# Attention level in one burst of eight tiles, a new beginning and a new weight decoding, in a fused attention and double MLP kernel

## Chip, cores and metric

The kernel runs on one core of one Trainium2 chip. The core has a matrix engine (TensorE, PE), three engines for elementwise work (VectorE, DVE; ScalarE, ACT; GpSimd, POOL) and a queue that issues transfers (SyncE, SP); each runs its own list of instructions in order, and they wait for each other by semaphores. On-chip memory (SBUF) and the accumulators of PE (PSUM, eight banks of 2 KB per partition) have 128 partitions. The metric is the device time of one run in microseconds (us).

## What is computed

A chunked linear attention with decay, then two MLPs on its 3072 tokens of 256 features, in float32 (the weights arrive as float64).

```python
batch, H, S, D, N, chunk = 4, 8, 768, 32, 16, 32
for c in range(S // chunk):                       # state: (batch, H, N, D), zero at first
    cum = np.cumsum(log(clip(a, 1e-06, 1.0))[chunk c], axis=-1)
    L = np.exp(cum[..., :, None] - cum[..., None, :]) * causal
    M = np.einsum('bhin,bhjn->bhij', Cc, Bc) * L
    y[chunk c] = einsum('bhij,bhjd->bhid', M, xc) + einsum('bhin,bhnd->bhid', Cc, state) * np.exp(cum)[..., None]
    state = exp(sum(la)) * state + sum_j(Bc_j xc_j * exp(cum[-1] - cum_j))
x = y.transpose(0, 2, 1, 3).reshape(3072, 256)
h = np.maximum(x @ w_in, 0.0)                     # first MLP: 256 -> 2048 -> 256
x = h * h @ w_out
h = x @ w2_in                                     # second MLP, same sizes
y = (h * np.clip(h + 3.0, 0.0, 6.0) / 6.0) @ w2_out
```

## The kernel before

**Tiles and steps.** The 3072 tokens are six tiles of 512. The attention runs in 12 levels of 64 positions for all four batches and eight heads; two levels make one tile's input (act_h and act_l, the high part in the PE's reduced format and the rest of it). The first MLP ("a") goes through the six tiles, then the second ("b"). One tile has 16 steps f, one for each 128 of the 2048 hidden features. `step` (L411) emits: `mm1` (L350), six matmuls of 128x128 by 128x512 into a bank h (high weight by high input, low weight by high, high weight by low, for two halves of the 256 features); `gate` (L362); and `mm2` (L383) of the step two back (LAG = 2), six matmuls into the two output banks y. After step 15 each output is copied to act_h on ACT (L399) and subtracted from on DVE (L400) to give act_l. Everything is scheduled by hand: each engine executes in the order in which the program emits.

**Gate.** For "a": Relu and Square on ACT, a rounding copy gh on DVE (L369), and gl = g - gh on DVE (L377). For "b": Relu(h + 3) on ACT (L372), min and multiply on DVE (L373), copy on ACT (L374), gl on DVE.

**Weights.** Each MLP has 16 blocks j of 0.5 MB, taking turns between w_in and w_out; steps 2n and 2n+1 need blocks 2n and (two steps later) 2n+1. `load_w` (L286) decodes a block: its transfer, `early` (L313, ACT copies the upper words of the float64s), two DVE operations that collect low bits and sign (L332, L334), a third that joins them (L336), and `late` (L301): the high part on ACT (L306), the low part on POOL (L307). It is a generator that the steps advance: twice a step in tile 0 for the first MLP's weights, and from tile 5 on for the second's, with three transfer buffers each.

**Attention of one level.** `scale` (POOL) multiplies B and C by the decays and lays C out by head; `tokens` (POOL) scales the token-major B; `scores` (L216) are 16 small matmuls on 32 rows; `mask` (L226, DVE) moves the causal part of them to `mt`; `outputs` (L234) has 16 matmuls C by state ("inter", L241) and 32 mask by x ("intra", L247); `update` (L252) has 16; `advance` (DVE) makes the next state from u and the decay gam; `evac` writes the level into the tile's input (ACT L280, DVE L282). These small matmuls sit four at a time in separate parts of the PE array, and a level comes to PE in three visits: scores in step 2, outputs in step 4, update in step 5 of each period of eight steps (`PLAN`, `ORDER`). While tile t is in the MLP, levels 2t+2 and 2t+3 are worked; levels 0 and 1 stand in the beginning.

**Beginning.** DVE forms the running products of the decays a (`products`), their reciprocals and corrections (`decays`, in two halves), PE spreads them over the partitions for levels 0 and 1 (`spread`, L149), and the others go through DRAM (scr). The decays of a whole level (gl) make a round trip through DRAM as well (`gammas_out`, L162 and L163), before `gammas` (L167) can run on DVE.

**Banks.** In the first MLP: one pool for the attention with two banks for scores or outputs ("cy") and one for the update, two banks for h, three for y.

The lines on which the change and the sum turn are these: the order in which a decode alternates with a step, and the banks.

```python
ps_h = ctx.enter_context(tc.tile_pool(name="ps_h", bufs=2, space=PSUM, reuse_waits="tile"))
ps_y = ctx.enter_context(tc.tile_pool(name="ps_y", bufs=3, space=PSUM, reuse_waits="tile"))
```

Of the kernel before, what the change touches and what calls it, by code (L numbers as in the profile page):

```python
# [46 lines left out]
def attn_mlp_mlp(ctx: ExitStack, tc, a, bT, cT, bK, x, w1i, w1o, w2i, w2o, yT):  # L47
# [21 lines left out]
    act_h, act_l = ([actp.tile([P, 2, TOK], F32R, tag=f"{k}{i}", name=f"act_{k}{i}") for i in range(NT)] for k in "hl")  # L69
# [8 lines left out]
    mts = [at1.tile([P, 2, 2 * G], F32, tag=f"mt{i}", name=f"mt{i}") for i in range(2)]  # L78
# [30 lines left out]
    ef = at1.tile([R0, 2, G], F32, tag="efr", name="efr")  # L109
    gs = at1.tile([R0, 3, CPG], F32, tag="gs", name="gs")  # L110

    ft = at1.tile([CH, CPG, NB, SGS, H], F32, tag="ft", name="ft")

    gl = at1.tile([P, 2, NB, NLEV], F32, tag="gl", name="gl")
    gam = at1.tile([P, 2, NB, NLEV], F32, tag="gam", name="gam")
    pr, rc = ef[:, 0, :], ef[:, 1, :]
    p4 = pr.rearrange("p (c e t) -> p c e t", e=2, t=SEG)
    r4 = rc.rearrange("p (c e t) -> p c e t", e=2, t=SEG)
    scr = dram.tile([CPG, SGS, H, 2, NB, CH], F32, tag="scr", name="scr")
    gsc = dram.tile([H, 2, NGRP, CPG], F32, tag="gsc", name="gsc")  # L120

    def products():
        nc.vector.tensor_scalar(out=av, in0=av, scalar1=1e-6, scalar2=1.0, op0=ALU.max, op1=ALU.min)
        nc.vector.tensor_copy(out=seg.rearrange("p (s t) -> p s t", t=SEG)[:, :, 0:1],
                              in_=av.rearrange("p (s t) -> p s t", t=SEG)[:, :, 0:1])
        nc.vector.tensor_tensor_scan(out=pr, data0=av, data1=seg, initial=1.0, op0=ALU.mult, op1=ALU.max)
        for i in range(2):
            nc.vector.tensor_copy(out=gs[:, i, :], in_=p4[:, :, i, SEG - 1])

    def decays(i):  # L130

        t, k = slice(i * P, i * P + P), slice(2 * i, 2 * i + 2)
        nc.vector.reciprocal(out=rc[:, t], in_=pr[:, t])
        nc.vector.tensor_copy(out=gs[:, 2, k], in_=r4[:, k, 0, SEG - 1])
        nc.vector.tensor_tensor(out=r4[:, k, 0, :], in0=r4[:, k, 0, :],
                                in1=gs[:, 0, k].unsqueeze(2).broadcast_to([R0, 2, SEG]), op=ALU.mult)
        nc.vector.tensor_tensor(out=p4[:, k, 0, :], in0=p4[:, k, 0, :],
                                in1=gs[:, 2, k].unsqueeze(2).broadcast_to([R0, 2, SEG]), op=ALU.mult)

    def decays_out(i):  # L140
        for k in (2 * i, 2 * i + 1):
            for w in range(2):
                nc.sync.dma_start(out=scr[k, :, :, w].rearrange("s h b t -> b (s h) t"), in_=ef[:, w, k * CH:k * CH + CH])

    def spread(l):

        efp = ps_s.tile([P, NB, 2, CH], F32, tag=f"efp{l}", name=f"efp{l}")
        for b in range(NB):
            nc.tensor.matmul(out=efp[:, b], lhsT=sel[:, b], rhs=ef[:, :, l * CH:l * CH + CH], start=True, stop=True)  # L149
        lev[l]["ef"] = efp.rearrange("p b w t -> p w b t")  # L150

    def f_tokens(i):

        ftp = ps_s.tile([CH, 2, R0], F32, tag="ftp", name=f"ftp{i}")
        for j in range(2):
            nc.tensor.transpose(out=ftp[:, j, :], in_=rc[:, (2 * i + j) * CH:(2 * i + j + 1) * CH],
                                identity=ident[0:R0, 0:R0])
        nc.scalar.copy(out=ft[:, 2 * i:2 * i + 2].rearrange("p k b s h -> p k (b s h)"), in_=ftp)

    def gammas_out():  # L160
        for i in range(2):
            nc.sync.dma_start(out=gsc[:, i].rearrange("h g k -> g h k"), in_=gs[:, i, :])  # L162
        nc.sync.dma_start(out=gl.rearrange("p i b l -> p (i b l)"), in_=gsc.rearrange("h i g k -> h (i g k)")  # L163
                          .unsqueeze(1).broadcast_to([H, NS, 2 * NGRP * CPG]))

    def gammas():
        nc.vector.tensor_tensor(out=gl[:, 1, :, 0:NLEV - 1], in0=gl[:, 1, :, 0:NLEV - 1], in1=gl[:, 0, :, 1:NLEV],  # L167
                                op=ALU.mult)
        for e in range(2):
            nc.vector.tensor_scalar(out=gam[:, e], in0=gl[:, 1], scalar1=hm[:, e:e + 1], scalar2=None, op0=ALU.mult)  # L170
# [380 lines left out]
```

## Time and profile before

| | |
|---|---|
| median of 3 runs | 629.55 us (627.54 to 629.99) |
| the profiled execution | 629.27 us, its span 627.6 us |
| PE busy | 588.6 us, 94% of the span |
| DVE busy | 370.8 us, 59% |
| ACT busy | 296.8 us, 47% |
| POOL busy | 100.8 us, 16% |
| moved by transfers | 34.58 MB, mean 55 GB/s |

The span is the time between the first and the last instruction of the profiled execution; busy times count instructions that compute, not waits or issues. The chain of waits is followed backwards from the last instruction, at each step to what released it, and here it is read forwards; a timeline lists every instruction of a stretch with its start; the releaser behind an arrow is what ended the idle time before it. PEclk is the clock that PE was granted, as a share of its full speed.

### The profile page before, as it was taken

What the parts mean: (1) busy time and instruction counts of PE and PEld (TensorE: products, weight loads), DVE (VectorE), ACT (ScalarE), POOL (GpSimd) and SP (SyncE); (2) the same over time, 40 slices, a digit from 0 to 9 for tenths busy, and PEclk for the clock granted to TensorE, in tenths of its full rate; (3) what the DMA queues carried; (4) which work ended last, traced back from release to release, by engine and by line L of the source; (5) the groups of instructions that cost most, each with busy time, mean ns of one, the idle gap of its engine ahead of it and who ended that gap; (6) DMA issues with size and microseconds to landing.
All of it is one profiled execution on the core that took longest, in us unless ns stands there. A gap on an engine that the chain in (4) does not pass through costs nothing.

```text
span 627.6 us, 10383 instructions
## 1 busy us (share of the span) xinstructions
PE 588.6 (94%) x4180; PEld 474.2 (76%) x4180; DVE 370.8 (59%) x589; ACT 296.8 (47%) x494; POOL 100.8 (16%) x95
## 2 busy tenths in 40 slices
PE   4646879999999999999999999999999999999997
PEld 4534657787787888878887788888888888888885
DVE  4548899645543644445389988454555555554543
ACT  1216545343444434443476666554544544545453
POOL 5143465221020120200013323000000000000000
PEclk9777899999999999999999999999999999999999
DMA  8493732113021130500024430010000100100101
GB/s 201 118 200 110 181 105 68 36 43 76 9 68 36 45 75 9 169 1 1 2 68 137 132 101 1 1 34 0 18 17 1 35 1 1 33 1 1 34 0 35
DMA packets 36081, 34.58 MB, mean 55 GB/s; under 512 B 15200, under 2 KB 30656, under 8 KB 36032
## 3 DMA queue, kind: packets, MB, share of 16 engines
q1 hardware_dynamic: 36032, 33.91, 20.7%
q8 instruction: 33, 0.54, 0.4%
q14 instruction: 16, 0.13, 0.1%
HBM read 30.56 MB, written 3.35 MB: 54 GB/s over the span
## 4 chain that ended last, share of the span: by engine, by line
PE 82%; DVE 7%; DMA 4%; issue 3%; ACT 1%; POOL 1%; SPq 1%; DVEq 0%; ACTq 0%
PE yb L394 21%; PE hb L356 21%; PE ya L394 18%; PE ha L356 17%; PE ya L247 2%; DMA rawa<-in_w1i 2%; DVE gla L377 2%; PE sc L222 1%; DMA gsc<-gs 1%; PE ya L241 1%; DVE lowa L333 1%; DVE wta L336 1%; POOL al L307 1%; DMA C<-in_cT 1%; PE u L259 1%
## 5 line engine op out<-in xcount | busy, mean ns | idle before, releaser
L366 ACT ACTIVATE ga<-ha 128x512 f32<-128x512 f32 x96 | 57.2, 596 | 127.4 <-PE ha L356 124.9
L377 DVE TENSOR_TENSOR glb<-gb,ghb 128x512 fp32r<-128x512 f32 x96 | 66.4, 691 | 60.5 <-ACT ghb L374 60.1
L373 DVE SCALAR_TENSOR_TENSOR gb<-gb,hb 128x512 f32<-128x512 f32 x96 | 66.1, 688 | 54.1 <-ACT gb L372 53.7
L374 ACT ACTIVATE ghb<-gb 128x512 fp32r<-128x512 f32 x96 | 60.8, 633 | 74.8 <-DVE gb L373 74.8
L372 ACT ACTIVATE gb<-hb,three 128x512 f32<-128x512 f32 x96 | 65.9, 686 | 51.9 <-PE hb L356 51.9
L369 DVE CAST gha<-ga 128x512 fp32r<-128x512 f32 x96 | 43.6, 454 | 74.8 <-ACT ga L367 74.8
L377 DVE TENSOR_TENSOR gla<-ga,gha 128x512 fp32r<-128x512 f32 x96 | 83.9, 874 | 6.7
L356 PE MATMUL ha<-act_h,al 128*128 128x512 f32 x192 | 77.2, 402 | 9.5 <-POOL al L307 9.5
L356 PE MATMUL ha<-act_h,ah 128*128 128x512 f32 x192 | 76.9, 400 | 7.6 <-ACT ah L306 4.8
L394 PE MATMUL ya<-gla,ah 128*128 128x512 f32 x192 | 75.8, 395 | 3.7 <-DVE gla L377 3.7
L394 PE MATMUL ya<-gha,ah 128*128 128x512 f32 x192 | 78.5, 409 | 0.0
L356 PE MATMUL ha<-act_l,ah 128*128 128x512 f32 x192 | 76.2, 397 | 0.0
L394 PE MATMUL ya<-gha,al 128*128 128x512 f32 x192 | 75.3, 392 | 0.0
L394 PE MATMUL yb<-glb,bh 128*128 128x512 f32 x192 | 74.8, 390 | 0.0
L356 PE MATMUL hb<-act_h,bl 128*128 128x512 f32 x192 | 74.7, 389 | 0.0
L394 PE MATMUL yb<-ghb,bl 128*128 128x512 f32 x192 | 74.7, 389 | 0.0
L394 PE MATMUL yb<-ghb,bh 128*128 128x512 f32 x192 | 74.7, 389 | 0.0
L356 PE MATMUL hb<-act_h,bh 128*128 128x512 f32 x192 | 74.7, 389 | 0.0
L356 PE MATMUL hb<-act_l,bh 128*128 128x512 f32 x192 | 74.7, 389 | 0.0
L367 ACT ACTIVATE ga<-ga 128x512 f32<-128x512 f32 x96 | 60.6, 632 | 3.0
L356 PEld LDWEIGHTS ha<-act_h,al 128*128 128x128 f32 x192 | 36.9, 192 | 18.8 <-POOL al L307 11.3
L356 PEld LDWEIGHTS ha<-act_h,ah 128*128 128x128 f32 x192 | 36.7, 191 | 17.7 <-ACT ah L306 6.6
(81 smaller groups left out, 745.5 us busy)
## 6 DMA issues: line engine op xcount, KB each, us to landing
x<-in_x SPq DMA_DIRECT2D x24, 256.0 KB
rawa<-in_w1i SPq DMA_DIRECT2D x8, 512.0 KB
rawa<-in_w1o SPq DMA_DIRECT2D x8, 512.0 KB
rawb<-in_w2i SPq DMA_DIRECT2D x8, 512.0 KB
rawb<-in_w2o SPq DMA_DIRECT2D x8, 512.0 KB
out_yT<-o SPq DMA_DIRECT2D x12, 256.0 KB
ef<-scr SPq DMA_DIRECT2D x10, 256.0 KB
B<-in_bT SPq DMA_DIRECT2D x12, 128.0 KB
```

The source lines that it names most:

```text
L222: nc.tensor.matmul(out=sc[r:r + CH, p // 2, b * P:b * P + P].rearrange("j (e i) -> j e i", e=2), lhsT=d["B"][q, b], rhs=d["cb"][q, :, b], ...
L241: nc.tensor.matmul(out=y[r:r + CH, p // 2, b * CH:b * CH + CH], lhsT=state["S"][q, b], rhs=d["C"][q, b], start=b == 0, stop=False, skip_gr ...
L247: nc.tensor.matmul(out=y[o:o + HD, p // 2, b * CH:b * CH + CH], lhsT=d["x"][j, b, HD * h:HD * h + HD], rhs=mts[l % 2][j, p // 2, (2 * b + ...
L356: nc.tensor.matmul(out=h, lhsT=wt[fb][:, k, fo * P:fo * P + P], rhs=xt[t][:, k, :], start=i == 0, stop=i == 5)
L366: nc.scalar.activation(out=g, in_=h, func=AF.Relu)
L367: nc.scalar.activation(out=g, in_=g, func=AF.Square)
L369: nc.vector.tensor_copy(out=gh, in_=g)
L372: nc.scalar.activation(out=g, in_=h, func=AF.Relu, bias=three)
L373: nc.vector.scalar_tensor_tensor(out=g, in0=g, scalar=6.0, in1=h, op0=ALU.min, op1=ALU.mult)
L374: nc.scalar.activation(out=gh, in_=g, func=AF.Copy)
L377: nc.vector.tensor_tensor(out=gl, in0=g, in1=gh.bitcast(F32), op=ALU.subtract)
L394: nc.tensor.matmul(out=ys[m], lhsT=terms[i][0][fb][:, fo, m * P:m * P + P], rhs=terms[i][1], start=f == 0 and i == 0, stop=f == NF - 1 and ...
```

## The change

- **Level in a burst.** `outputs` and `update` of a level and the scores of the next level become one visit to PE, `burst`, in step 4 of each eight. The operands lie so that batches 0 and 1 use rows 0 to 63 and batches 2 and 3 rows 64 to 127 (x and B of tokens in one buffer `xb` of two halves): matmuls of 32 or 64 rows stand eight at a time in the array. Inter becomes 32 matmuls of 32 columns of weights instead of 16 of 64. All results of a level lie in one buffer of four banks ("att"), so the outputs y keep two banks instead of three. `after` in step 5 has the evacuation, the next level's mask and the state. The layout of C by head moves from POOL to ACT (`heads`).
- **Beginning.** The decays of levels 0 to 2 come by a matmul (`gammas_first`), those of later levels by the round trip, taken in at step 5 of tile 0. Scores of levels 0 and 1 go together. B of levels 0 and 1 and one part of xb are issued by ACT. The decays go out to DRAM in 4 transfers instead of 8, behind their second half. Block 2 comes behind level 2's inputs, block 3 behind the write of the decays.
- **Weight decoding.** Blocks 3 to 10 land in the space of the inputs of tiles 2 to 5, which are not used yet, so that transfers run further ahead (two at each even step of tile 0). The first two of the three DVE operations now have one source each and no mixed operation (`join`). The order within a step is `decode`: join(j), early(j+1), split(j), with j = f + 3 in tile 0; for the second weights, by the table `at`, one block in two of three steps.
- **Gate of the first MLP.** Relu on ACT, g = Relu(h) times h on DVE, the rounding copy on ACT, gl on DVE: as in the second MLP.

```diff
-PLAN = {"load": (0, 0), "scale": (0, 0), "tok": (1, 0), "scores": (2, 0), "mask": (2, 0), "out": (4, 0), "upd": (5, 0),
-        "evac": (5, 0)}
+PLAN = {0: {1: ("load3",), 2: ("scale2",), 3: ("head2",), 4: ("scores2", "mask2", "tok2"), 6: ("scale3", "head3"),
+            8: ("burst2",), 9: ("evac2", "load4"), 10: ("tok3",), 11: ("scale4", "head4"), 13: ("burst3",),
+            14: ("evac3", "load5")}}
...
+        _d = {0: (f"tok{_l}",), 1: (f"scale{_l + 1}",), 2: (f"head{_l + 1}",), 4: (f"burst{_l}",),
+              5: (f"evac{_l}",), 6: (f"load{_l + 2}",)}
...
+    def gammas_first(ps):
+
+        nc.vector.tensor_tensor(out=gg, in0=gs[:, 1, 0:CPG - 1], in1=gs[:, 0, 1:CPG], op=ALU.mult)
+        gp = ps[:, 0:NB * (CPG - 1)].rearrange("p (b l) -> p b l", b=NB)
+        for b in range(NB):
+            nc.tensor.matmul(out=gp[:, b], lhsT=sel[:, b], rhs=gg, start=True, stop=True)
+        return gp
...
+    def scores(l, sc):
...
+        for c in range(2):
+            for p in range(NPR):
+                for r in range(2):
+                    q, b = slice(32 * p, 32 * p + 32), 2 * r + c
+                    nc.tensor.matmul(out=sc[CH * r:CH * r + CH, p, P * c:P * c + P].rearrange("j (e i) -> j e i", e=2),
+                                     lhsT=d["bc"][q, b, 1], rhs=d["cb"][q, :, b], start=True, stop=True)
...
+    def intra(l):
+
+        y, x = lev[l]["y"], lev[l]["xb"]
+        for c in range(2):
+            for k in range(2):
+                for r in range(2):
+                    q = slice(CH * r, CH * r + CH)
+                    for o in range(4):
+                        h = 4 * k + o
+                        p, e = divmod(h, 2)
+                        nc.tensor.matmul(out=y[HD * o:HD * o + HD, 2 * r + k, c * CH:c * CH + CH],
+                                         lhsT=x[q, c, HD * h:HD * h + HD],
+                                         rhs=mts[l % 2][q, p, (2 * c + e) * CH:(2 * c + e) * CH + CH],
+                                         start=not l, stop=True, skip_group_check=True)
...
+    def burst(l, nxt=True):
+
+        t = ps_a.tile([P, NPR, TOK], F32, tag="att", name=f"att{l}")
+        place(l, t)
+        inter(l)
+        intra(l)
+        update(l)
+        if nxt and l + 1 < NLEV:
+            scores(l + 1, t[:, :, 0:G])
+
+    def after(l):
+        evac_h(l)
+        if l + 1 < NLEV:
+            mask(l + 1, (1,))
+        advance(l)
+        evac_l(l)
+        if l + 1 < NLEV:
+            mask(l + 1, (0,))
...
+        def dma(self, j):
+            if self.pre == "a" and 3 <= j < 11:
+                t, k = 2 + (j - 3) // 2, "hl"[(j - 3) % 2]
+                raw = actp.tile([P, 2, 256, 2], U32, tag=f"{k}{t}", name=f"rawa{j}")
...
+            nc.vector.tensor_scalar(out=low, in0=self.raws[j][:, :, 1], scalar1=0x80000000, scalar2=None,
+                                    op0=ALU.bitwise_and)
+            nc.vector.tensor_scalar(out=low.bitcast(U16).rearrange("p (n z) -> p n z", z=2)[:, :, 0], in0=top,
+                                    scalar1=2.0 ** -13, scalar2=7.0, op0=ALU.mult, op1=ALU.min)
...
-            nc.scalar.activation(out=g, in_=g, func=AF.Square)
...
-            nc.vector.tensor_copy(out=gh, in_=g)
...
+            nc.vector.tensor_tensor(out=g, in0=g, in1=h, op=ALU.mult)
...
+        nc.scalar.activation(out=gh, in_=g, func=AF.Copy)
...
-    ps_y = ctx.enter_context(tc.tile_pool(name="ps_y", bufs=3, space=PSUM, reuse_waits="tile"))
+    ps_y = ctx.enter_context(tc.tile_pool(name="ps_y", bufs=2, space=PSUM, reuse_waits="tile"))
...
+    def decode(x, j):
+
+        if j < NF:
+            x.join(j)
+        if j + 1 < NF:
+            x.early(j + 1)
+        if j < NF:
+            x.split(j)
+
+    def mid_first(t, f):
+        for j in (6 + 2 * (f // 2) + i for i in range(2)) if f % 2 == 0 else ():
+            if j < NF:
+                w1.dma(j)
+        if f == 5:
+            gammas()
+        attention(t, f)
+        decode(w1, f + 3)
...
+            at = {(k * 3 + 1) // 2 + 1: k for k in range(NF)}
```

What this does to the order on three engines is shown here; a name's number only tells its instances apart.

**PE, level 4 in tile 1.** Before, behind the last `mm1` matmul of step 4 stood two sorts of small matmuls (L241 inter, L247 intra); the scores (L222) stood two steps ahead, and the update (L259) one step behind:

```order
L356 MATMUL ha_4_1236<-act_l_93,ah_538 128x512
L241 MATMUL ya_1248<-C_738,S_1059 64x64 x16
L247 MATMUL ya_1248<-mt_104,x_742 32x64 x32
L394 MATMUL ya_0_1208<-gha_2_1182,ah_493 128x512
L394 MATMUL ya_0_1208<-gha_2_1182,al_494 128x512
```

After, inter (L295), intra (L309), update (L323) and the next level's scores (L275) stand in the same place:

```order
L437 MATMUL ha_4_1278<-act_l_887,ah_506 128x512
L295 MATMUL att_1291<-bc_891,S_1144 32x64 x32
L309 MATMUL att_1291<-mt_92,xb_894 32x64 x32
L323 MATMUL att_1291<-xb_894 32x64 x16
L275 MATMUL att_1291<-cb_1246,bc_1150 64x128 x16
L471 MATMUL ya_0_1250<-gha_2_1240,ah_472 128x512
```

Update and scores moved into the one visit, and inter has twice as many matmuls of half the columns.

**ACT, steps 0 and 1 of tile 0.** L366 is the gate's Relu and L367 its Square, L306 the high part of a block (late), L315 a block's first copy (early). Before:

```order
L366 ACTIVATE ga_0_454<-ha_0_445 128x512
L367 ACTIVATE ga_0_454<-ga_0_454 128x512
L306 ACTIVATE ah_466<-wta_393 128x512
L315 ACTIVATE wta_470<-rawa_427 128x512
L366 ACTIVATE ga_1_484<-ha_1_475 128x512
```

After, with L447 the Relu, L452 the gate's rounding copy, L402 early and L421 the high part (split); block 3's early (rawa_423) stands ahead of the first Relu:

```order
L402 ACTIVATE wta_440<-rawa_423 128x512
L447 ACTIVATE ga_0_458<-ha_0_449 128x512
L452 ACTIVATE gha_0_456<-ga_0_458 128x512
L402 ACTIVATE wta_470<-rawa_425 128x512
L421 ACTIVATE ah_472<-wta_440 128x512
L447 ACTIVATE ga_1_486<-ha_1_477 128x512
```

The high part now stands behind the next block's early and belongs to the block joined in the same step, not to the one joined the step before.

**SP, the transfers from the decays on.** Before, the level decays (gsc, gl) and eight writes of scr stood ahead of block 3 (rawa_320), and level 2's inputs behind it:

```order
L162 DMA gsc<-gs 12x8x4 x2
L163 DMA gl<-gsc 128x1x96
L143 DMA scr<-efr 4x24x64 x8
L297 DMA rawa_320<-in_w1o 128x1024
L182 DMA B_404<-in_bT 128x4x64
L182 DMA C_406<-in_cT 128x4x64
L186 DMA ef_408<-scr 128x1x512
L193 DMA x_410<-in_x 64x4x256 x2
```

After, level 2's inputs and block 2 (rawa_166) have been issued already; four writes, then blocks 3 to 5, the level decays, level 2's decays and two more blocks:

```order
L396 DMA rawa_166<-in_w1i 128x1024
L156 DMA scr<-efr 4x24x128 x4
L396 DMA rawa_423<-in_w1o 128x1024
L396 DMA rawa_425<-in_w1i 128x1024
L396 DMA rawa_427<-in_w1o 128x1024
L195 DMA gl<-gsc 128x1x96
L236 DMA ef_430<-scr 128x1x512
L396 DMA rawa_462<-in_w1i 128x1024
L396 DMA rawa_464<-in_w1o 128x1024
```

The writes still stand ahead of block 3, but each carries both halves of a level's decays, and four more blocks follow without a level's inputs between them.

## Rows read from the trace of the kernel before

**Rows 1.** Chain of waits in order of time: start us, us, what.

```profile
36.96 9.93 DMA rawa<-in_w1i
...
106.89 1.36 PE ha L356 x6
...
312.31 1.36 PE ha L356 x6
...
359.01 1.37 PE hb L356 x6
...
619.09 4.09 PE yb L394 x18
```

**Rows 2.** Timeline to 50 us: start us, us, engine, line, operation, [idle before <-releaser].

```profile
5.84 2.05 PE L149 MATMUL efp<-efr,sel 96*128 96x128 f32 x8 [5.84 <-DVE efr L137]
...
19.69 5.12 SPq L143 DMA_DIRECT2D scr<-efr  x8
...
21.12 0.20 DVE L167 TENSOR_TENSOR gl<-gl 128x44 f32<-128x44 f32 x1 [4.76 <-DMA gl<-gsc]
...
28.96 0.79 PE L356 MATMUL ha<-act_h,ah 128*128 128x512 f32 x1
...
41.94 1.93 PE L222 MATMUL sc<-cblk,B 32*64 32x128 f32 x32
...
46.97 0.66 ACT L315 ACTIVATE wta<-rawa 128x512 f32<-128x512 f32 x1 [12.35 <-DMA rawa<-in_w1i]
```

**Rows 3.** The chain of waits again, level 6 in tile 2.

```profile
165.43 1.03 PE sc L222 x32
...
172.15 0.62 PE ya L241 x32
172.77 1.03 PE ya L247 x64
...
176.74 0.58 PE u L259 x32
```

**Rows 4.** Busy us by stretch: PE, PEld, DVE, ACT, POOL, PEclk, DMA share, GB/s.

```profile
40.00:42.00 2.00, 2.00 (x9) 1.06 (x9) 0.00 (x0) 0.00 (x0) 0.47 (x1) 0.50 1.10 186
90.00:100.00 10.00, 7.34 (x148) 5.45 (x148) 9.90 (x16) 5.96 (x11) 4.84 (x3) 1.00 0.22 55
```

**Rows 5.** Timeline: a tile's evacuation (164 us) and a second-MLP gate (450 us).

```profile
163.92 1.07 ACT L399 ACTIVATE act_h<-ya 128x512 fp32r<-128x512 f32 x2
...
450.06 0.39 PE L356 MATMUL hb<-act_l,bh 128*128 128x512 f32 x1
...
450.55 0.69 ACT L372 ACTIVATE gb<-hb,three 128x512 f32<-128x512 f32 x1 [0.64 <-PE hb L356]
...
451.27 0.69 DVE L373 SCALAR_TENSOR_TENSOR gb<-gb,hb 128x512 f32<-128x512 f32 x1 [0.64 <-ACT gb L372]
...
451.99 0.63 ACT L374 ACTIVATE ghb<-gb 128x512 fp32r<-128x512 f32 x1 [0.76 <-DVE gb L373]
```

**Rows 6.** Groups by line and shape: count | busy us, mean ns | idle before <-releasers.

```profile
L366 ACT ACTIVATE ga<-ha 128x512 f32<-128x512 f32 x96 | 57.2, 596 | 127.4 <-PE ha L356 124.9 <-DVE gla L377 2.4
...
L307 POOL TENSOR_TENSOR al<-wta,ah 128x512 fp32r<-128x512 f32 x16 | 27.0, 1690 | 50.8 <-ACT ah L306 50.8
...
L229 DVE COPY_PREDICATED mt<-tri,sc 128x512 f32<-128x512 uint32 x24 | 16.3, 732 | 7.8 <-PE sc L222 7.6
...
L282 DVE TENSOR_TENSOR act_l<-ya,act_h 128x256 fp32r<-128x256 f32 x24 | 9.1, 419 | 35.3 <-ACT act_h L280 35.3
...
L332 DVE TENSOR_SCALAR lowa<-rawa 128x512 uint32<-128x512 uint16 x16 | 7.5, 470 | 0.1
...
L133 DVE RECIPROCAL efr<-efr 96x128 f32<-96x128 f32 x2 | 1.9, 936 | 0.0
```

**Rows 7.** Timeline at 331 us, GpSimd and VectorE.

```profile
330.96 1.81 POOL L307 TENSOR_TENSOR bl<-wtb,bh 128x512 fp32r<-128x512 f32 x1 [3.03 <-ACT bh L306]
...
331.54 1.78 DVE L377 TENSOR_TENSOR gla<-ga,gha 128x512 fp32r<-128x512 f32 x1
```

More of the change, by code (lines that the diff above doesn't have):

```diff
@@ L145, in spread, with decays_out @@
-    def spread(l):
-        efp = ps_s.tile([P, NB, 2, CH], F32, tag=f"efp{l}", name=f"efp{l}")
+    def decays_out():
+        for k in (2, 3, 0, 1):
+            nc.sync.dma_start(out=scr[k].rearrange("s h b w t -> b (s h) (w t)"),
+                              in_=ef[:, k].rearrange("p w t -> p (w t)"))
+    def spread(l, efp):
         for b in range(NB):
-            nc.tensor.matmul(out=efp[:, b], lhsT=sel[:, b], rhs=ef[:, :, l * CH:l * CH + CH], start=True, stop=True)
-        lev[l]["ef"] = efp.rearrange("p b w t -> p w b t")
@@ L454, in attn_mlp_mlp @@
-    decays_out(1)
-    scores(0)
-    mask(0)
-    update(0)
-    outputs(0, ps_s, "ya0")
-    gammas()
-    next(w1)
-    scores(1)
-    advance(0)
-    evac(0)
-    mask(1)
-    next(w1)
-    outputs(1)
-    update(1)
-    next(w1)
-    evac(1)
-    advance(1)
-    for l in (2, 3):
-        load(l)
-        load_x(l)
-    next(w1)
-    next(w1)
+    gammas_first2(gp)
+    sc = ps_a.tile([P, NPR, TOK], F32, tag="att", name="att_s")
+    scores(0, sc[:, :, 0:G])
+    scores(1, sc[:, :, G:])
+    w1.early(0)
@@ new lines, in attn_mlp_mlp @@
+    mask(0, (0, 1))
+    mask(1, (0, 1))
+    place(0, ps_s.tile([P, 4, TOK], F32, tag="big", name="yu0"))
+    update(0)
+    intra(0)
+    advance(0)
+    evac_h(0)
+    w1.join(0)
+    w1.split(0)
+    w1.early(1)
+    evac_l(0)
+    burst(1, False)
+    evac_h(1)
+    w1.join(1)
+    evac_l(1)
+    advance(1)
+    decays(1)
+    decays_out()
+    f_tokens(1, ps_s.tile([P, 4, TOK], F32, tag="big", name="ftb")[:, 2])
+    w1.split(1)
+    w1.early(2)
+    for j in (3, 4, 5):
+        w1.dma(j)
@@ L476, in attn_mlp_mlp @@
+    gammas_in()
+    load_ef(2)
+    w1.join(2)
+    w1.split(2)
+    w1.early(3)
     start_ctx.close()
     ps_h = ctx.enter_context(tc.tile_pool(name="ps_h", bufs=2, space=PSUM, reuse_waits="tile"))
-    ps_y = ctx.enter_context(tc.tile_pool(name="ps_y", bufs=3, space=PSUM, reuse_waits="tile"))
+    ps_y = ctx.enter_context(tc.tile_pool(name="ps_y", bufs=2, space=PSUM, reuse_waits="tile"))
     yps, hps = [ps_y], [ps_h]
-    does = {"load": lambda l: l + 2 < NLEV and (load(l + 2), load_x(l + 2)), "scale": lambda l: scale(l, nc.gpsimd),
-            "tok": tokens, "scores": scores, "mask": mask, "out": outputs, "upd": lambda l: (update(l), advance(l)),
-            "evac": evac}
@@ L484, in attn_mlp_mlp, with first_scores @@
-    PLAN["load"] = (6, 0)
-    def mid(t, f):
-        l, i = 2 * t + 2 + f // 8, f % 8
-        if l < NLEV:
-            for nm in ORDER:
-                if PLAN[nm][0] == i:
-                    does[nm](l)
+    def first_scores(l):
+        sc = ps_a.tile([P, NPR, TOK], F32, tag="att", name=f"att_s{l}")
+        scores(l, sc[:, :, 0:G])
+    does = {"load": load_all, "scale": scale, "head": heads, "tok": tokens, "scores": first_scores, "mask": mask,
+            "burst": burst, "evac": after}
@@ L493, in attn_mlp_mlp @@
     w2 = None
+    at = {}
     for t in range(NT):
```

373 lines of the change are left out of this document (198 added, 175 removed).

## The prediction

> **What bounds the kernel now.** I read the chain of waits first [rows 1]: where TensorE (PE) never waits it is pieces of six matmuls of 1.36 us, so a step (first matmul group and second) is 2.72 us, a tile of 16 steps 43.5, and the 192 steps of both MLPs 522. The same view gives borders: tile 1 begins at 106.89, tile 5 at 312.31, the second MLP at 359.01, the last 18 matmuls end at 623.18; the first MLP matmul starts at 28.96 [rows 2]. So the span of 627.6 is 29.0 of beginning, 77.9 for tile 0 (34.4 above 43.5), 205.4 for tiles 1 to 4 (31.3 above 174.1), 46.7 for tile 5 (3.2 above), 264.2 for the second MLP (97 steps are 263.8: nothing to gain) and 4.4 of end. The run took 629.27, 1.67 more than its span; I sum against that run, and the median, 629.55, is 0.28 above it.
>
> In tiles 1 to 4 the excess is the attention's own matmuls: per level pieces of 1.03, 0.62, 1.03 and 0.58 [rows 3], 3.26 together, and 0.7 that three visits to another tile shape cost: 31.3 is seven levels of 4.0 and the last, which has no update, of 3.1. In tile 0 it is the weights: ScalarE (ACT) idled 12.35 us before it could copy block 4 [rows 2], whose transfer took 9.93 [rows 1], and step 1's Relu stood behind that copy, so not before 47.5. The granted clock is part of it: 0.50, 1.2 GHz, at 40 to 42 us, 1.00 at 90 to 100 with PE busy 7.3 of 10 [rows 4].
>
> **The change part by part.**
>
> *Burst.* The small matmuls are bound by streaming through four tiles, not by their issue: 64 of 64 columns take 1.03, 32 take 0.58, so one more costs 14 ns; with 128 columns it is twice that [rows 3]; and at 1.2 GHz the scores took 1.93 [rows 2, 4]. Eight tiles at a time therefore halve scores (0.52), intra (0.52) and update (0.29); inter has twice the matmuls at twice the width: 0.62. Sum 1.95, plus one visit (0.22) and two changes of shape inside (0.06 to 0.1 each): 2.3 where 4.0 stood, and 1.45 for 3.1 in the last level. Tiles 1 to 4: 7 x 2.3 + 1.45 = 17.6 instead of 31.3, so -13.7. The bound on the other side: no more than four tiles ever ran, so no row shows eight; were 14 ns an issue limit, scores, intra and update would stay and inter would double to 1.07: 4.1 a level and 2.4 for the last, 31.1 in all, so -0.2.
>
> [...]
>
> *Two output buffers instead of three* (the burst needs four PSUM banks). At the start of tiles 1 to 4 the first second-MLP-group matmul must wait until the previous tile's output 0 is evacuated. From the gate's timeline [rows 5], counted from the last matmul start of step 1 (there 450.06): Relu begins at +0.49 and, with the first MLP's 0.60 [rows 6], ends at +1.09, multiply (0.69) at +1.81, copy (0.63) at +2.47, the subtraction gl, as long as the multiply, at +3.19; the evacuating subtraction stands behind gl on VectorE (DVE), 0.69 more: +3.9. PE would be there at +0.23 + 1.36 + 1.36 = +2.95. So a stall of 0.95 and 0.1 to restart, four times: +4.2. Output 1 is free just in time. Between 0 (if evacuation overtook the gate; the order forbids it) and 8.
>
> *Beginning.* Matrix gammas replace the DMA round trip for which DVE idled 4.76 [rows 2]; scores for two levels go together. But the second spread waits for f_tokens and the gamma matmuls: the first ends at 5.84 + 2.05 [rows 2], 16 records between them at 0.13 to 0.26 each (a spread's eight take 2.05) are 2.1 to 4.1, I take 2.5, the second spread 2.05, scale 0.69, two gamma operations 0.5: 13.6. From there DVE works in a row: four masks of 0.73, an advance of 0.42, two joins of 1.55, four evacuations of 0.42, a second advance 0.85, a reciprocal 0.94 and three small operations of the second decays, 0.7 [rows 6]: 2.9 + 0.4 + 3.1 + 1.7 + 0.85 + 1.6 = 10.6, and about 1.3 for waits: the second decays end at 25.5 (22.5 to 27.5). What is queued behind them: on PE f_tokens and then the first MLP matmul, at about 26.5 against 28.96. On SP the four scr writes (0.64 each, 2.6 [rows 2]), and behind them block 3. It is issued at 28.1; alone it should land 3.6 later (between 2.5, its 0.5 MB at 200 GB/s, and 9.93 [rows 1]). On ACT block 3's copy (0.67, estimated from L366's 0.60) stands ahead of the first Relu: Relu 0 at 32.4, Relu 1 one loop later, some 11 us before today's 47.5.
>
> *Decode loop of tile 0.* In steps 0 to 12 ACT has Relu(f), copy(f), early, split of block f+3, Relu(f+1); DVE has multiply(f), the three join operations, gl(f). Split waits for the join, and the next Relu stands behind split: a loop that no lead of PE shortens. Relu 0.60 [rows 6], multiply 0.69 [rows 5], join 0.42 + 0.42 + 0.69 [rows 5, 6], three hand-overs 0.1 and gaps 0.06, and 0.53 from split's start to the next Relu's (two ACT operations 1.07 [rows 5]): 3.5. GpSimd's subtraction for the block (1.69 [rows 6]) starts as split ends and runs till 1.85 after the Relu began; the join's first operation is due at 1.32. A DVE operation that comes while GpSimd runs may wait: gla took 1.78 instead of 0.69 and ended 0.55 after the POOL operation [rows 7]. So 3.5 to 4.1; I take 3.8, since most operations of the nearest kind (L332, mean 0.47 [rows 6]) did not wait. [...]
>
> 13 steps: 49.4. Attention in the loop on DVE: two masks of 0.73 in step 4, three small gamma operations in step 5 (0.6), and in step 9 two masks, four operations of 0.42 (advance and low parts): 1.5 + 0.6 + 3.1 = 5.2. Three scales and two token products on POOL, hitting DVE for 0 to 1.1 each: 3.0. From Relu 13 to tile 1: mm2 11 to 13, mm1 14 and 15 and the evacuation at step 14 ahead of gl: 5.3. Tile 1 begins at 32.4 + 49.4 + 5.2 + 3.0 + 5.3 = 95.3, 11.6 earlier (88 to 104).
>
> *Second weights.* The same order is used in 16 of 24 steps from tile 5 on. Of three steps two decode: 3.5 and, behind the other's POOL operation, 3.8; the third needs only Relu, multiply and copy, 1.95. 9.25 against 8.16 of PE: 1.1 lost in each of eight groups, 8.7, plus two tile evacuations in the chain, 1.3 each; about 3 is hidden by the lead that gl has over its use. +7.5 (3 to 11) replaces today's 3.2 to 3.5: +4.1.
>
> At nothing: the gate's new operations (ACT and DVE have the same sum, and 1.3 of 2.72 busy; without that cover 0.1 per step), head masks on ACT, the evacuation in step 5 of a level: 2.9 of DVE ahead of gl, which is due 3 us later; if that cover went, up to 0.7 in each of eight levels.
>
> **Sum.** 95.3 + (205.4 - 13.7 + 4.2 = 195.9) + (46.7 + 264.2 + 4.1 = 315.0) + 4.4 = 610.6; with 1.67 around it 612.3.
>
> **Rivals.** *Eight tiles don't overlap*: the burst costs 4.1 and 13.5 come back: 625.8. For it: nothing ever ran more than four. Against: time follows columns and clock. *The loop is quicker*: no POOL collision (13 x 0.3 + 3.0), block 3 lands at 30 and the second weights hide: 612.3 - 3.9 - 3.0 - 1.7 - 4 = 600. *The join meets GpSimd twice* (the slower side): in every block, of both MLPs, not only the first but also the last join operation waits 1.1, because GpSimd's subtraction comes late; 29 blocks x 1.1 = 32: 644, slower than now from 0.7 a block on. Against: GpSimd is idle from 1.85 on until the join is done, except for five scales and products. *The clock stays at 1.2 GHz in tile 0*: steps of 5.44 instead of 3.8, 13 x 1.64 = 21: 633.6. For it: 0.50 after idle stretches [rows 4]; against: with PE busy for 7.3 of 10 it was 1.00, and here it is 2.72 of 3.8.
>
> **How the numbers follow.** Forecast 612.3 with 0.62, quicker loop 0.17, no overlap 0.10, join twice 0.05, slow clock 0.06. The range leaves out the two slow cases and the tails of the others: the unknown terms (loop +-4, transitions +-4, second weights +-4, beginning +-3) give 603 to 622 around the forecast, and I reach to both neighbours: 601 to 625. A measurement of this kernel tells 0.5% (3.1 us) from no change: faster means below 626.4, slower above 632.7. Faster takes forecast, quicker loop and half of no overlap (it lies on that bound): 0.84; same its other half and a third of the slow clock: 0.07; slower the rest: 0.09.
>
> **What would show it.** Right: a burst of 2.3 us with scores of about 0.5; tile 1 beginning near 95; Relu 0 behind block 3's copy at about 32 and Relus 3.8 apart; a PE wait of about 1 us on act_l at the start of tiles 1 to 4; 7 us of waits at the second weights. Wrong: small matmuls still 14 ns apart, a step in tile 0 that PE sets (2.72), or blocks that come later than the loop asks.

## The result and the profile after

The changed kernel takes 638.13 us (median of 4 runs, 635.36 to 640.41) against 629.77 us for the kernel before on the same chips (4 runs): a ratio of 1.0146, 95% interval 1.0108 to 1.0183. It is slower by 8 us (1.1 to 1.8%) where I forecast 17 us less, and it lies outside the range of 601 to 625. The profiled execution took 636.95 us with a span of 635.2.

Three lines of the page of the changed kernel: busy time of each engine, shares of the chain of waits by engine, and the queue that carries instructions (packets, MB, share of 16 engines).

```profile
PE 583.9 (92%) x4552; PEld 467.5 (74%) x4552; DVE 363.0 (57%) x590; ACT 304.2 (48%) x521; POOL 69.3 (11%) x73
...
PE 64%; DVE 15%; ACT 6%; issue 6%; DMA 4%; SPq 3%; POOL 1%; DVEq 0%; ACTq 0%; POOLq 0%
...
q8 instruction: 35, 0.57, 0.4%
```

PE is busy 5 us less than before, so the small matmuls did get shorter, and yet its share of the chain fell from 82% to 64%: DVE has 15% (7% before), and 6% (3%) stand under "issue", waiting for which the profile names nobody. The borders, from the timeline (start us, us, engine, line, operation, [idle before <-releaser]):

```profile
29.46 0.79 PE L437 MATMUL ha<-act_h,ah 128*128 128x512 f32 x1 [0.57 <-ACT ft L174]
...
99.15 0.50 PE L437 MATMUL ha<-act_h,ah 128*128 128x512 f32 x1 [0.17 <-ACT act_h L349]
...
315.62 0.39 PE L437 MATMUL ha<-act_h,ah 128*128 128x512 f32 x1
...
362.36 0.39 PE L437 MATMUL hb<-act_h,bh 128*128 128x512 f32 x1
```

These answer to [rows 1, 2]. The last matmul ends at 630.83.

| part | before | predicted | after |
|---|---|---|---|
| first MLP matmul starts | 28.96 | 26.5 | 29.46 |
| tile 1 begins | 106.9 | 95.3 | 99.15 |
| tiles 1 to 4 | 205.4 | 195.9 | 216.5 |
| tile 5 and second MLP | 310.9 | 315.0 | 315.2 |
| end | 4.4 | 4.4 | 4.4 |

So the miss of 24.6 us in the span is 3.9 before tile 1 and 20.6 in tiles 1 to 4.

**Tiles 1 to 4, by step.** A step without attention is 2.72; the four tiles have 42.4 us above that, where I expected 21.8. By the starts of the steps they are: 20.9 for the eight bursts where nothing disturbs them (2.73 each, 1.79 for the last); 8.3 for gaps inside or right behind four of the bursts, and 0.9 for a slow clock after one of them; 5.1 for a wait in the third step behind the burst, where gl of the step next to it is used; 4.6 for the start of each tile; 2.4 for a backlog that tile 0 leaves to tile 1. A disturbed burst, that of level 6, in the chain of waits (start us, us, what), which answers to [rows 3]:

```profile
168.36 0.79 PE att L295 x53
169.15 0.79 PE att L309 x53
169.93 0.31 PE att L323 x22
170.25 2.05 issue
172.30 0.70 PE att L275 x32
```

Inter 0.79, intra 0.79, update 0.31, and then PE does nothing for 2.05 us before the scores. The other gaps of that kind in these tiles, from PE's timeline:

```profile
144.68 0.40 PE L471 MATMUL ya<-gha,al 128*128 128x512 f32 x1 [0.90 <-issue]
...
251.63 0.44 PE L275 MATMUL att<-cb,bc 32*64 32x128 f32 x5 [1.71 <-issue]
...
279.44 0.31 PE L323 MATMUL att<-xb 64*32 64x64 f32 x6 [1.98 <-issue]
```

They come at different instructions: behind the burst of level 5, between update and scores at level 6, between two scores at level 9, between two update matmuls at level 10; levels 4, 7, 8 and 11 have none. Operands hardly explain a gap in the middle of one group. Counting every instruction of PE in the trace from the start (weight loads, matmuls and the 48 of its sequencer, most of them waits for semaphores), the gaps stand at instructions 3009, 3521, 5313 and 5825, and one of 1.0 us in the beginning at 705: all distances are multiples of 256. The instruction queue of the page moved 0.57 MB in 35 pieces, 16 KB each, for some 9,150 instructions: one piece for about 260. The trace has the time of each piece (us), and counted from the start the 11th, 13th, 20th and 22nd belong to the gaps:

| level | instruction | its piece | PE goes on | behind the piece's end |
|---|---|---|---|---|
| 5 | 3009 | 142.29 to 143.23 | 144.68 | 1.44 |
| 6 | 3521 | 169.44 to 170.88 | 172.30 | 1.42 |
| 9 | 5313 | 249.35 to 250.28 | 251.63 | 1.35 |
| 10 | 5825 | 276.72 to 278.00 | 279.44 | 1.44 |

Each of these pieces begins only 0.7 to 1.4 us after PE has passed the place 256 instructions earlier. Wherever in tiles 1 to 4 PE crosses such a place without a gap, the piece had ended 2.7 us or more before.

A burst of inter, intra, update and scores is 384 records (loads and matmuls) in 2.5 us. Where one such place falls into its first third, the next falls inside the burst or right behind it, 1.5 to 1.8 us later by PE's records at the four gaps, before its piece is there. At level 7 a place falls right at the burst's start; there the next piece began at 193.50, ahead of the burst at 195.7, and no gap came.

### The profile page after: what moved, and what is told of

It reads as the page before. It is cut to its first block, busy times and chain, and to the rows that moved or that the text cites. A ratio compares the mean times of both kernels' runs of the same rounds, so it can differ in the third digit from the quotient of the medians.

```text
span 635.2 us, 11105 instructions
## 1 busy us (share of the span) xinstructions
PE 583.9 (92%) x4552; PEld 467.5 (74%) x4552; DVE 363.0 (57%) x590; ACT 304.2 (48%) x521; POOL 69.3 (11%) x73
## 4 chain that ended last, share of the span: by engine, by line
PE 64%; DVE 15%; ACT 6%; issue 6%; DMA 4%; SPq 3%; POOL 1%; DVEq 0%; ACTq 0%; POOLq 0%
PE yb L471 19%; PE hb L437 19%; PE ya L471 11%; PE ha L437 11%; DVE ga L448 3%; DVE mt L283 2%; DVE gla L454 2%; ACT ga L447 2%; ACT gha L452 2%; DMA rawa<-in_w1o 2%; DVE wtb L411 1%; PE att L295 1%; PE att L309 1%; DVE act_l L354 1%; DVE lowb L409 1%
## 5 line engine op out<-in xcount | busy, mean ns | idle before, releaser
L452 ACT ACTIVATE gha<-ga 128x512 fp32r<-128x512 f32 x96 | 60.8, 633 | 99.8 <-DVE ga L448 99.8
L448 DVE TENSOR_TENSOR ga<-ga,ha 128x512 f32<-128x512 f32 x96 | 65.7, 685 | 73.3 <-ACT ga L447 72.7
L452 ACT ACTIVATE ghb<-gb 128x512 fp32r<-128x512 f32 x96 | 60.9, 634 | 72.9 <-DVE gb L451 72.9
L454 DVE TENSOR_TENSOR gla<-ga,gha 128x512 fp32r<-128x512 f32 x96 | 67.8, 707 | 44.8 <-ACT gha L452 44.8
L471 PE MATMUL ya<-gla,ah 128*128 128x512 f32 x192 | 78.1, 407 | 9.7 <-DVE gla L454 9.5
L447 ACT ACTIVATE ga<-ha 128x512 f32<-128x512 f32 x96 | 56.7, 591 | 52.1 <-PE ha L437 52.1
L471 PEld LDWEIGHTS ya<-gla,ah 128*128 128x128 f32 x192 | 36.7, 191 | 25.1 <-DVE gla L454 16.6
```

Of the source, the lines that this page charges most:

```text
L447: nc.scalar.activation(out=g, in_=h, func=AF.Relu)
L448: nc.vector.tensor_tensor(out=g, in0=g, in1=h, op=ALU.mult)
L452: nc.scalar.activation(out=gh, in_=g, func=AF.Copy)
L454: nc.vector.tensor_tensor(out=gl, in0=g, in1=gh.bitcast(F32), op=ALU.subtract)
L471: nc.tensor.matmul(out=ys[m], lhsT=terms[i][0][fb][:, fo, m * P:m * P + P], rhs=terms[i][1], start=f == 0 and i == 0, stop=f == NF - 1 and ...
```

## Experiments

**Is it the supply of instructions?** The first experiment moves only the count of instructions.

```diff
     spread(1, efp)
+    for i in range(32):
+        q = slice(32 * (i % 4), 32 * (i % 4) + 32)
+        nc.tensor.matmul(out=big[q, 2, 256:288], lhsT=ident[q, q], rhs=ident[q, q], start=True, stop=True)
     scale(0, nc.vector)
```

> The changed kernel with 32 extra matmuls of 32x32 in the beginning, written to an unused part of a bank; they shift every later PE instruction by 128 records (two loads and two matmuls each). Theory A: PE's instructions come in blocks of 256, and a burst that uses up one block within about 3 us waits for the next; the gaps without a releaser then move from the bursts of levels 5, 6, 9 and 10 to those of levels 4, 7 and 8 (1 to 2 us each; level 5 at most 0.5). Theory B: the scores at the burst's end wait for their operands (the laid out C, the scaled B); the gaps then stay at levels 5, 6, 9 and 10. Time by A within 3 us of the changed kernel, by B the same plus up to 1 us.

639.52 us in a single run. PE's timeline of this kernel at the bursts of levels 4, 5, 7 and 8:

```profile
119.98 0.43 PE L275 MATMUL att<-cb,bc 32*64 32x128 f32 x3
121.89 0.69 PE L275 MATMUL att<-cb,bc 32*64 32x128 f32 x29 [1.48 <-issue]
...
147.74 0.69 PE L275 MATMUL att<-cb,bc 32*64 32x128 f32 x32
...
201.53 0.37 PE L275 MATMUL att<-cb,bc 32*64 32x128 f32 x2 [1.54 <-issue]
...
230.60 0.42 PE L323 MATMUL att<-xb 64*32 64x64 f32 x3 [1.93 <-issue]
```

Levels 4, 7 and 8 now have the gap, levels 5, 6, 9 and 10 none; the gaps stand at instructions 2497, 4289 and 4801, the same remainder of 256 as before, and PE goes on 1.37 to 1.50 us behind the end of a piece. Two more came in tile 0, at levels 2 and 3 (1.59 and 1.02) and at the same remainder, which I had not worked out. Apart from 1 us that the padding adds to the beginning, nothing but the count was changed ahead of these bursts, so theory A holds, and theory B falls.

**Fewer records in a row.** The cure that follows is to leave the next piece more time: inter and intra in step 4, update and scores in step 5. This kernel also moves a part of DVE's work from step 5 to step 6 (the next one moves a similar part, and nothing else).

```diff
         intra(l)
+        if not nxt:
+            update(l)
+        lev[l]["t"] = t
+
+    def after(l):
         update(l)
-        if nxt and l + 1 < NLEV:
-            scores(l + 1, t[:, :, 0:G])
-
-    def after(l):
+        if l + 1 < NLEV:
+            scores(l + 1, lev[l]["t"][:, :, 0:G])
         evac_h(l)
+        evac_l(l)
+
+    def rest(l):
         if l + 1 < NLEV:
-            mask(l + 1, (1,))
+            mask(l + 1)
         advance(l)
-        evac_l(l)
...
```

> The kernel with the spread work (the first mask and the state also in step 6, the low parts in step 5) and with a level's burst in two visits: inter and intra in step 4, update and the next level's scores in step 5. Theory A (blocks of 256 instructions): 256 and 128 records with a step between them use up at most one block in 3 us; the gaps in the bursts go (8.3 us in tiles 1 to 4 down to under 1.5), eight more visits cost 0.25 to 0.3 each, 2.2, and the late gl goes as in the kernel with the spread work alone: 11 to 12 us less than the changed kernel, total about 627. Theory B (operands): the scores come 2.7 us later, so their gap shrinks too, but the gaps at the update (level 10) and behind the burst (level 5) stay: 630 to 632.

624.76 us, ratio to the kernel before 0.9925 (0.9892 to 0.9959). That is 8.6 less than the kernel that moves DVE's work alone (633.39, ten runs of each), so the second visit, and not the moved work, brought most of that. Level 6 in its chain of waits:

```profile
166.05 0.78 PE att L295 x53
166.83 0.79 PE att L309 x53
167.62 1.58 PE ya L474 x6
...
170.58 0.39 PE att L323 x32
170.97 0.62 PE att L275 x32
```

No gap is left in any level of tiles 1 to 4; a level costs 1.79 + 1.25 = 3.04 everywhere, 0.31 for the second visit, and no wait stands in the third step behind it. That is 2 us better than expected; the slow clock behind the gaps went as well (1.00 from 100 to 300 us). That clock, in the changed kernel, by the view of stretches (columns as in [rows 4]):

```profile
277.00:279.40 2.40, 0.46 (x47) 0.30 (x31) 0.74 (x2) 0.63 (x1) 0.00 (x0) 1.00 0.00 0
...
282.00:285.00 3.00, 3.00 (x10) 2.29 (x9) 0.00 (x0) 0.00 (x0) 0.00 (x0) 0.61 0.00 0
```

PE was busy 0.46 of 2.40 us there (level 10's gap), and from 282 to 285 the granted clock was 0.61 with PE busy throughout (0.50 from 281 to 284, 1.00 from 284.5); that cost 0.9. Behind the gaps of levels 5, 6 and 9 it stayed at 1.00.

**The wait behind a burst.** In the changed kernel, the chain behind level 4's burst:

```profile
122.33 0.64 ACT gha L452
122.97 0.54 ACT act_h L349 x2
...
123.53 0.75 DVE mt L283
...
124.95 0.75 DVE act_l L354 x2
125.70 0.66 DVE mt L283
126.36 1.00 DVE gla L454
127.36 0.04 issue
127.40 1.20 PE ya L471 x4
```

gl of step 5 stands behind two masks, the state and the low parts on DVE, and these behind the evacuation copies on ACT, which stand behind the gate's rounding copy. PE waits for gl. At three of the seven levels gl itself, 0.69 alone, took 0.4 to 0.5 longer while GpSimd worked, here beside the next level's tokens:

```profile
126.18 0.61 POOL L264 TENSOR_TENSOR xb<-xb,ft 128x256 f32<-128x256 f32 x1
...
126.25 1.09 DVE L454 TENSOR_TENSOR gla<-ga,gha 128x512 fp32r<-128x512 f32 x1
```

At a fourth, level 6, an operation of the state took 0.69 instead of 0.43 in the same way. These meetings are 1.6 of the 5.1; at the three levels without one PE waited 0.5. Two kernels try the wait from two sides. The first moves the low parts and one mask to step 6:

> The changed kernel with the second half of the work behind a burst (the low parts on DVE, and the second mask) moved from step 5 of a level to step 6 (level 3 excepted). Theory A: the 3.1 us of DVE work in one step make gl late, PE waits 0.5 to 1.05 us for it two steps later in each level; spread over two steps the waits go: 5 to 6 us less in tiles 1 to 4, total about 632. Theory B: PE waits because the multiply, which now reads h from PSUM, holds one of two banks; then nothing changes, 638. The gaps in the bursts (8 us in four levels) stay by both.

The second has the old gate:

```diff
             nc.scalar.activation(out=g, in_=h, func=AF.Relu)
-            nc.vector.tensor_tensor(out=g, in0=g, in1=h, op=ALU.mult)
+            nc.scalar.activation(out=g, in_=g, func=AF.Square)
+            nc.vector.tensor_copy(out=gh, in_=g)
...
-        nc.scalar.activation(out=gh, in_=g, func=AF.Copy)
+            nc.scalar.activation(out=gh, in_=g, func=AF.Copy)
...
```

The rounding copy on ACT stays for the second MLP alone.

> The changed kernel with the old gate in the first MLP: Relu and Square on ACT, rounding copy and gl on VectorE. Theory A (the prediction): the gate's form costs nothing in tiles 1 to 4, apart from the waits for a late gl behind each burst, which shrink a little since VectorE has 0.24 less a step: between 0 and 3 us less there; in tile 0 the loop has ACT's Square (0.55) in it instead of the multiply (0.6 to 0.7), and the rounding copy stands behind it: plus or minus 3 us. Total 635 to 641. Theory B: the multiply's second read of h from PSUM holds the h bank 0.7 us longer and is itself what makes PE wait: 5 us or more less, 633 or below.

With the work spread: 633.39 us (0.3 to 1.0% above the kernel before), and of the 5.1 us of waits 0.7 is left, while the gaps and the slow clock stayed and were even longer (10.8 instead of 9.2). With the old gate: 634.39 us (0.6 to 1.3% above), between the two theories' totals; 0.8 is left of the waits, though tile 0 became 2.2 longer. Its timeline at the same burst:

```profile
124.56 0.60 ACT L447 ACTIVATE ga<-ha 128x512 f32<-128x512 f32 x1 [4.21 <-PE ha L437]
125.19 0.63 ACT L448 ACTIVATE ga<-ga 128x512 f32<-128x512 f32 x1
125.73 0.63 ACT L349 CAST act_h<-att 128x256 fp32r<-128x256 f32 x2
...
129.09 0.67 DVE L455 TENSOR_TENSOR gla<-ga,gha 128x512 fp32r<-128x512 f32 x1
```

From Relu to the evacuation copies it is 1.17 us here and 1.89 in the changed kernel, where ACT waits between the two for DVE's multiply. So the wait belongs to both edits together, the new gate and the work of a whole level in one step, and either alone takes it away. The bank theory fails: in the changed kernel PE waited for the multiply once, 1.9 us, in tile 0.

**The start of a tile.** The tile evacuation ahead of the rounding copy:

```diff
             nc.vector.tensor_tensor(out=g, in0=g, in1=h, op=ALU.mult)
+            yield
...
         gt = gate(pre, t, f, h)
+        next(gt)
+        if pre == "a" and t and f == 1:
+            mm2(*pend.pop(0))
         next(gt)
         if mid:
```

> The changed kernel with the first MLP's tile evacuation (copies on ACT, subtractions on VectorE) ahead of the rounding copy and gl of step 1 of the next tile, instead of behind them. Theory A: PE waits at the start of tiles 1 to 4 for the subtraction of output 0, 1.0 to 1.4 us each, since only two output buffers are left; the subtraction then ends some 1.4 us earlier and the waits go: 4 us less, about 634. Theory B: another wait takes the place (gl of step 1 comes 1.9 us later, or the h bank is not free): less than 1.5 us.

635.86 us. The 1.04 us at the start of tiles 2 to 4, and 1.44 of tile 1, are gone (the steps there are 2.72 to 2.75), as by theory A. Of the 4.6 us the total shows half: 2.3, less than the 4 us expected, and hardly to be told from nothing by four runs of each. In its profiled execution the gaps, the waits behind the bursts and the backlog (3.5 instead of 2.4 in tile 1) came out longer.

**Two queues in the beginning and tile 0.** In tile 0 of the changed kernel ACT waits once for a level's inputs:

```profile
78.76 0.33 SPq L396 DMA_DIRECT2D rawa<-in_w1o  x1
...
83.23 0.61 SPq L236 DMA_DIRECT2D ef<-scr  x1
...
87.78 1.28 POOL L249 TENSOR_TENSOR bc<-ef,bc 128x512 f32<-128x512 f32 x1 [2.35 <-DMA ef<-scr]
...
89.09 0.91 ACT L258 ACTIVATE cb<-bc,hm 128x256 f32<-128x256 f32 x2 [3.16 <-POOL bc L249]
```

On SP the transfer of block 15 waits until 78.76 for a buffer, level 4's inputs stand behind it, the scaling waits for them, ACT's layout for the scaling, and the next Relu stands behind that.

```diff
+    for j in (3, 4, 5):
+        w1.dma(j)
     decays(0)
...
-    for j in (3, 4, 5):
-        w1.dma(j)
     gammas_in()
...
-PLAN = {0: {1: ("load3",), 2: ("scale2",), 3: ("head2",), 4: ("scores2", "mask2", "tok2"), 6: ("scale3", "head3"),
-            8: ("burst2",), 9: ("evac2", "load4"), 10: ("tok3",), 11: ("scale4", "head4"), 13: ("burst3",),
+PLAN = {0: {1: ("load3",), 2: ("scale2",), 3: ("head2",), 4: ("scores2", "mask2", "tok2"), 6: ("scale3", "head3"), 7: ("load4",),
+            8: ("burst2",), 9: ("evac2",), 10: ("tok3",), 11: ("scale4", "head4"), 13: ("burst3",),
```

> The changed kernel with transfers in another order on SP: blocks 3 to 5 right behind block 2 instead of behind the decays' write, and level 4's inputs in step 7 instead of step 9, ahead of the transfers of blocks 14 and 15, which wait there for their buffers. Theory A: Relu 0 no longer stands behind block 3's copy and starts at about 32.3 instead of 35.5; the 4.0 us for which ACT and DVE waited at 87 to 91 us for level 4's decays go but for 0.5; together 6 to 6.6 us less in tile 0, total about 632. Theory B: the decode loop of 3.6 us a step takes the gain back or the early blocks delay the decays of level 2 (scale in step 2) by as much: less than 2 us.

636.44 us, and tile 1 begins at 96.77, 2.4 earlier instead of 6. The second edit did its part:

```profile
33.50 0.63 ACT L421 ACTIVATE ah<-wta 128x512 fp32r<-128x512 f32 x1 [1.38 <-DVE wta L411]
...
34.72 0.60 ACT L447 ACTIVATE ga<-ha 128x512 f32<-128x512 f32 x1
...
85.56 0.91 ACT L258 ACTIVATE cb<-bc,hm 128x256 f32<-128x256 f32 x2 [0.96 <-POOL bc L249]
```

ACT waits 0.96 instead of 3.16. But Relu 0 starts at 34.72 and not at 32.3: with block 3 there, it stands behind block 2's high part, which is 1.5 later (33.50), because level 1's burst now has two gaps without a releaser, 0.76 and 1.48, where it had 1.02 before. They stand at instructions 449 and 705, the same remainder of 256; the piece for the first began at 19.25 instead of 17.83. The blocks' transfers run at that time; that they delay the piece is likely, but no run separates it.

**The decode loop and GpSimd.** One edit takes the high part out of the loop by making it a step later.

```diff
+        if j - 1 in x.wts:
+            x.split(j - 1)
         if j < NF:
             x.join(j)
         if j + 1 < NF:
             x.early(j + 1)
-        if j < NF:
-            x.split(j)
```

> The changed kernel with a block's high part (and so GpSimd's subtraction) made one decoding step later, ahead of the next block's join, in tile 0 and for the second weights. Theory A: the steps of tile 0 last 3.6 us because the next Relu stands behind a high part that waits for the join; without that wait VectorE's five operations set the step, 3.0 us: 7 us less in tile 0 and 4 to 6 us less at the second weights, total about 626. Theory B: VectorE's operations on SBUF and GpSimd's subtraction (1.3 us) do not run side by side whatever the order; the subtraction now meets the join's last operation or gl, and the step stays between 3.5 and 3.8: total 636 to 640.

647.0 us, worse than B's range. DVE and POOL in tile 0, from the timeline:

```profile
57.93 1.29 POOL L422 TENSOR_TENSOR al<-wta,ah 128x512 fp32r<-128x512 f32 x1 [3.59 <-ACT ah L421]
...
58.15 1.62 DVE L411 SCALAR_TENSOR_TENSOR wta<-wta,lowa 128x512 uint32<-128x512 uint32 x1
59.70 1.77 DVE L454 TENSOR_TENSOR gla<-ga,gha 128x512 fp32r<-128x512 f32 x1
...
59.18 1.73 POOL L249 TENSOR_TENSOR bc<-ef,bc 128x512 f32<-128x512 f32 x1
```

The join's last operation, 0.69 alone, ends 0.55 behind GpSimd's, and gl, 0.69 alone, 0.56 behind the next one. In the changed kernel the subtraction runs beside the multiply, whose second operand is in PSUM and which takes 0.69 even so (at 43.27, with GpSimd at work from 42.83 for 1.29), and most steps undisturbed by attention take 3.5 to 3.75 from Relu to Relu. So the loop is not what to break: it keeps GpSimd out of DVE's way.

**The second weights, thinner.** The same decoding, 16 blocks in 28 steps instead of 24 (`at = {(k * 9) // 5 + 1: k ...}`).

> The changed kernel with the second weights' blocks decoded in 16 of 28 steps (every 1.8 steps) instead of 16 of 24. Theory A: the loss of 7.7 us (3.2 in tile 5, 4.5 in the second MLP) is two decoding steps of 3.5 in a row, which a third step does not make up; with mostly one decoding step in two the sum of 3.5 and 2 us lies under 5.44 and the loss falls to 1 to 2 us: total about 632. Theory B: the loss is the single collision of a decoding step with what follows and stays per block: total 637 to 639.

634.44 us; the loss fell from 7.7 to 4.5 (1.4 in tile 5, 3.1 in the second MLP), not to 1 or 2, so it lies between the two theories. What is left stands mostly in the second MLP's first steps, where a decoding step meets tile 5's evacuation (1.1) and two decoding steps follow each other (0.9).

**All that helped.** Two visits, evacuation first, level 4's inputs in step 7, the thinner decoding, and level 3's masks and state moved from step 14 of tile 0 to step 2 of tile 1.

> The kernel with a level in two visits (624.8), with four more edits: the tile evacuation ahead of the rounding copy, the second weights spread to every 1.8 steps, level 4's inputs issued in step 7, and level 3's masks and state moved from step 14 of tile 0 to step 2 of tile 1. If the parts add as the traces of each show them (transitions 4 us, second weights 3, level 4's inputs 2, the backlog at the end of tile 0 about 2): 612 to 616. If one wait hides behind another there: 617 to 622.

614.29 us (613.70 to 614.82), ratio 0.9783 (0.9760 to 0.9805) to the kernel before: 2.0 to 2.4% faster than it, and faster than the changed kernel. Of its page and its chain of waits in tile 2:

```profile
PE 579.9 (95%) x4552; PEld 466.3 (76%) x4552; DVE 365.6 (60%) x590; ACT 305.8 (50%) x521; POOL 70.2 (11%) x73
...
161.06 0.78 PE att L296 x53
161.84 0.79 PE att L310 x53
162.63 1.58 PE ya L477 x6
164.21 1.38 PE ha L441 x6
165.59 0.39 PE att L324 x32
```

Tiles 1 to 4 take 197.8 us, and but for 0.5 at the start of tile 1 they have nothing above the steps but 1.79 + 1.25 a level. The parts added up. The same with the old gate:

> The same with the old gate (Relu and Square on ACT, rounding copy on VectorE) in the first MLP. The late gl behind the bursts is gone in both, so tiles 1 to 4 should be within 1 us of the kernel with the new gate; in tile 0 the old gate cost 2 us in the changed kernel (71.9 against 69.7) and should here too, less what the backlog at the end of tile 0 gives back: 612 to 618, within 3 us of the other.

614.67 us (0.9788, 0.9766 to 0.9810), no difference that can be told; tile 0 is 2.8 longer, tile 5 and the second MLP 1.1 shorter.

## Why the prediction was wrong

The step that failed is the cost of a burst, "Sum 1.95, plus one visit (0.22) and two changes of shape inside (0.06 to 0.1 each): 2.3 where 4.0 stood", together with the evacuation in step 5, which the sum put at nothing. In place of 2.3 a level the runs showed 2.73, gaps in half of the bursts that come from the supply of instructions, and a wait for gl behind seven of them.

- **The burst.** The matmuls of the new shapes come closer together, but not twice as close as forecast: intra 0.79 instead of 0.52, inter 0.79 instead of 0.62, scores 0.62 instead of 0.52; only the update halved (0.31). Why the others did not, no run shows. With the visit 2.73. That is 3.3 of the 20.6 us. 64 inter records in 0.79 us are 12.3 ns each, 32 of the update in 0.31 are 9.7.
- **What I had no term for.** I asked what the burst costs when it runs and not what feeds it: 384 records in 2.5 us. The gaps and the clock behind them are 9.2 us, the largest part of the miss. The profile of before had the instruction queue on its page (33 pieces for 8,360 records), and no level there put more than 192 small records in a row.
- **At nothing: "the evacuation in step 5 of a level: 2.9 of DVE ahead of gl, which is due 3 us later".** The cover was 0.5 us short, and 0.8 to 1.05 where GpSimd ran at the time: the evacuation begins behind the rounding copy, so DVE idles 1.2 us first. My bound of 0.7 a level was near (5.1 us in seven levels), but the central sum had zero. The same line put the gate at nothing, while the two edits make this wait together.
- **Two output buffers.** Right: 1.04 us at three tiles, 1.44 at one, 4.6 against 4.2, and the experiment took them away.
- **The beginning.** Relu 0 came at 35.5 instead of 32.4. I let DVE's chain end at 25.5; it ended at 28.0, through a gap of 1.0 in level 1's burst and a meeting of the join with GpSimd (1.40 for 0.47). Relu 0 stands behind block 3's copy, as I named it, for which ACT idled 2.2; with block 3 in time, in the kernel with two queues, it still came at 34.7, behind the decode of block 2.
- **The decode loop.** Right in cause: 3.5 to 3.75 a step against 3.8. That the total agrees too, 63.7 from Relu 0 to tile 1 against 62.9, is partly luck: in it stands a wait of 3.2 for level 4's inputs, which I did not see, because I costed the loop by its engines and did not follow SP past the transfer that waits for a buffer. The experiment showed that the order is also what keeps GpSimd's subtraction hidden. The clock rival did not come: steps of 3.6 are shorter than 5.44, and the granted clock, 0.50 at 50 to 54 us behind 4.4 us without a matmul, was 1.00 from 58 to 78. What the prediction calls 1.2 GHz is this 0.50: matmuls of 512 columns start 0.43 us apart there (52.22 to 53.92), so by an estimate 1.2 columns a ns, and 0.23 apart at 1.00 (58.17 to 59.99).
- **Second weights.** Right: +7.7 against +7.5. Where two decoding steps follow each other, a step mostly loses 0.9, and 1.3 where one meets tile 5's evacuation.

The prediction gave 0.09 to slower, all by rivals that did not occur; the slower result came from a mechanism that was not among them, plus a cover that was short and a burst of 2.73.

## What to carry to other kernels

Many small matmuls in a row can be limited by more than the array: count the instructions (weight loads too, and here two of each for a small float32 matmul: 32 of inter are 64 loads and 64 matmuls in the trace). Here 384 in a row in 2.5 us had gaps of 0.9 to 2.05 us in four of the seven such bursts of tiles 1 to 4; 256 and 128, with a step's large matmuls between them, had none. When an engine's order puts a level's follow-up in one step, work the cover out from when that work can start, not from its length alone. Before breaking a loop of waits, look at what it keeps apart.

## Not expected of the hardware

A gap that the profile puts down to nobody can be the supply of instructions: here 0.9 to 2.05 us, at every place the same remainder of 256 instructions, ended about 1.4 us behind a 16 KB piece, moved by padding and removed by a step of large matmuls in between. On SBUF operands, an operation of VectorE with a single source waited for GpSimd too: the uint16 operation of the join (0.47 alone) took 1.43 beside the scaling at 44.08 and 1.44 beside the one at 61.85.
